# Byte offsets of the rounded products' operands, and the down products in two groups (spectral filter and mixture of experts, one core)

## The chip, the cores and the metric

The kernel runs on one core of one Trainium2 chip. The metric is the time of one execution on the device in microseconds (us), as the median of several runs. TensorE (PE) multiplies; its weight loads (PEld) run beside its matmuls. VectorE (DVE), ScalarE (ACT) and GpSimd (POOL) work on tiles, and SyncE (SP) issues most transfers.

## The reference, cut to what matters

```
X = rfft(x, axis=1)                        # x: 8 batches x 2496 rows x 256
Yr = Xr @ w_r - Xi @ w_i + b_r             # Xr, Xi: real and imaginary part of X
Yi = Xr @ w_i + Xi @ w_r + b_i
Yr, Yi = soft_threshold(Yr, 0.01), soft_threshold(Yi, 0.01)
x = irfft(Yr + 1j * Yi, n=2496, axis=1)    # then 19968 tokens of 256
logits = x @ w_gate                        # 8 experts
e = argmax(logits); g = softmax(logits)[e]
out = g * (relu(x @ w1[e]) @ w2[e])        # w1: 256 x 1024, w2: 1024 x 256 per expert
```

## The kernel before, in words

The first 540 us are the spectral part. The transform of length 2496 = 39 x 64 is made of two short ones, both as matmuls. For each of 8 batches and 10 steps, `fwd_a` makes the first half of the forward transform, `fwd_b` the second, `mix` multiplies by `w_r`, `w_i - w_r` and `-w_i - w_r`, `inv_b`, `inv_z` and `inv_y` go back, and `gate_z`, `gate_y` and `route` choose an expert for each token and send its row to a list in memory. The rest is the expert part: 82 tiles of 256 tokens, each with an up product (`up`, L1081) and a down product (`down`, L1117 to L1120).

Products that must be more exact than one pass of rounded numbers gives are made of three: an operand is split into a rounded part (`h`, made by ACT in type float32r) and the rest (`l`, made by DVE), and PE adds up h·h, l·h and h·l. These are the **rounded products**. The ones with 256 moving columns are called narrow here, those with 512 wide:

- `mix` (L404): 18 narrow matmuls a step in 80 steps, 1440 in all. Weights of PE are `sh`, `sl`; the moving operands are `wh*`, `wl*`.
- `fwd_a` (L336): 3 wide for each of 66 pieces. Weights `fah`, `fal` (and `feh`, `fel`), moving `xah`, `xal`.
- `inv_y` (L491): 3 wide for each of 88 pieces. Weights `gh`, `gl`, moving `zh`, `zl`.
- `up`: 48 narrow a tile, in 4 groups of 12. Weights `h1`, `l1`, moving `xh2`, `xl2`. ACT then makes `hh` of a group, and DVE `hl`.
- `down`: two halves of 128 tokens (`h`), and in each, for 8 pieces `f`, one wide matmul that multiplies `hh` by both halves of `h2` (rounded and rest, 2 x 256 columns) and one narrow that multiplies `hl` by the rounded half. They stand alternately, the narrow one a piece behind.

Tiles are placed by pools, in the order in which the code asks for them, so a tile's byte offset in a partition follows from the sizes of those ahead of it. The order of PE, ACT, DVE and SP is the order of the code (a hand-written schedule in `spectral` and `finish_last`, then `step` tile after tile in `experts_rest`). Where a tile has a new expert, ACT and DVE split its weights first (`split1`, `split2`).

Of the kernel before, what the change touches and what calls it, by code (L numbers as in the profile page):

```python
# [10 lines left out]
F32 = mybir.dt.float32  # L11
# [88 lines left out]
class Kernel:  # L100
# [33 lines left out]
    def pool(self, st, name, bufs, side="left", **kw):  # L134
        return st.enter_context(self.tc.tile_pool(name=name, bufs=bufs, side=side, reuse_waits="tile", **kw))

    def open_inverse(self, st, pst):
        nc, nb = self.nc, self.nb
# [22 lines left out]
        self.gar = k.tile([120, 117], F32, name="gar")  # L161
        self.gh = k.tile([120, 117], F32R, name="gh")
        self.gl = k.tile([120, 117], F32R, name="gl")
        self.ids = k.tile([117, nb, G], I32, name="ids")
# [7 lines left out]
        self.mark = k.tile([1, 1], F32, name="mark")  # L172
        self.zf = [k.tile([128, 5288], F32, name=f"z{i}") for i in range(2)]
        self.zs = [z[:, 0:5280].rearrange("p (c n a) -> p c n a", c=2, n=66) for z in self.zf]

    def open_forward(self, st):
        tc, nc, nb = self.tc, self.nc, self.nb
        f = self.f = self.pool(st, "f", 1, side="right")
        self.xst = ExitStack()
        self.xp = self.pool(self.xst, "xp", 3)  # L180
        self.xh, self.xl = {}, {}
        self.tp = self.pool(st, "tp", 6, side="right")
# [18 lines left out]
        nc.sync.dma_start(self.fer, self.c_fe)  # L201
        self.wh, self.wl = {}, {}
        self.raw = {}
        self.nlam = f.tile([128, 1], F32, name="nlam")
# [42 lines left out]
    def split_weights(self):  # L247
        nc, f, raw = self.nc, self.f, self.raw
        ws = self.w.tile([128, 2, D], F32, tag="r", name="wsum")
        wd = self.w.tile([128, 2, D], F32, tag="r", name="wdif")  # L250
        raw["d"], raw["s"] = wd, ws

        def split(nm):
            self.wh[nm] = f.tile([128, 2, D], F32R, name="wh" + nm)
            self.wl[nm] = f.tile([128, 2, D], F32R, name="wl" + nm)
            nc.scalar.copy(self.wh[nm], raw[nm])
            nc.vector.tensor_sub(self.wl[nm], raw[nm], self.wh[nm])

        split("r")
        nc.vector.tensor_sub(wd, raw["i"], raw["r"])  # L260
        split("d")
        nc.scalar.copy(self.bias.rearrange("p a d -> p (a d)"), self.pbias)
        nc.vector.scalar_tensor_tensor(out=ws, in0=raw["i"], scalar=-1.0, in1=raw["r"], op0=ALU.mult, op1=ALU.subtract)
        split("s")
# [35 lines left out]
    def split_first(self):  # L300
        nc = self.nc
        self.fhl = []
        for nm, src in (("fa", self.far), ("fe", self.fer)):
            h = self.xp.tile(list(src.shape), F32R, name=nm + "h", bufs=1)
            l = self.xp.tile(list(src.shape), F32R, name=nm + "l", bufs=1)
            nc.scalar.copy(h, src)
            nc.vector.tensor_sub(l, src, h)
            self.fhl.append((h, l))
# [615 lines left out]
    def open_weights(self):  # L924
        self.xst.close()
        k2 = self.k2 = self.pool(self.top, "k2", 1)
        k2.tile([128, 144], F32, name="even")
        self.r1 = [k2.tile([128, F], F32, name=f"r1{q}") for q in range(2)]
# [116 lines left out]
    def upright(self, t):  # L1045
        if t >= self.nt:
            return
        nc = self.nc
        xf = self.w2p.tile([128, 2, 8, 32], F32, tag="xf", name="xf")
        nc.vector.transpose(xf.rearrange("p c t j -> p t c j"), self.xqs.pop(t))  # L1050
        yield
        xf = xf.rearrange("p c t j -> p c (t j)")
        xh = self.w2p.tile([128, 2, TT], F32R, tag="xh2", name="xh2", bufs=2)
        xl = self.w2p.tile([128, 2, TT], F32R, tag="xl2", name="xl2", bufs=2)
        with self.tc.high_priority():
            nc.scalar.copy(xh, xf)
        yield
        with self.tc.high_priority():
            nc.vector.tensor_sub(xl, xf, xh)
        self.xts[t] = (xh, xl)  # L1060

    def up(self, t, work=()):
# [4 lines left out]
        if t and self.psb:  # L1067
            self.split2(t)
        hh = self.w2p.tile([128, 8, TT], F32R, tag="hh", name="hh")
        hl = self.w2p.tile([128, 8, TT], F32R, tag="hl", name="hl")  # L1070
        for f2 in range(4):
# [26 lines left out]
    def down(self, t):  # L1098
# [9 lines left out]
        else:  # L1108
            at = [xr.bitcast(I32)[:, h, 1:2] for h in range(2)]
        o = self.w2p.tile([128, 2, D], F32, tag="o", name="o", bufs=2)  # L1110
        for h in range(2):
            p = self.psb.tile([128, 512], F32, tag="o", name="po") if self.psb else \
                self.psi.tile([128, 512], F32, tag="u", name="po", bufs=4)
            hs = slice(h * 128, (h + 1) * 128)
            for f in range(8):
                if f:
                    nc.tensor.matmul(p[:, :D], hl[:, f - 1, hs], w2[:, f - 1, 0, :], start=False, stop=False)  # L1117
                if f == 7:
                    nc.tensor.matmul(p[:, :D], hl[:, 7, hs], w2[:, 7, 0, :], start=False, stop=False)
                nc.tensor.matmul(p, hh[:, f, hs], w2[:, f].rearrange("p a d -> p (a d)"), start=f == 0, stop=f == 7)  # L1120
                if f == 3 and t < 2:
                    yield
            if not h:
# [67 lines left out]
```

## Time and profile before

| | |
|---|---|
| median of 3 runs | 1485.34 us (1484.37 to 1485.68) |
| profiled execution | 1484.46 us, its span 1482.6 us |
| PE busy | 1460.2 us, 98% of the span |
| DVE, ACT, POOL busy | 932.8, 772.3, 480.0 us |

A row of a timeline gives the start, the length, the engine, the line, the operation and its tiles, written as out<-in; for a matmul the first name after the arrow is the moving operand and the second PE's weights. Numbers at the ends of names are left out, so `h` stands for `h1` or `h2`, and `l` for `l1`. Matmuls overlap, so the time that one takes from PE is the step from its start to the next start, not its length.

### The profile page before, as it was taken

The numbers are of one execution on the slowest core, as the hardware profiler recorded it, in microseconds if no ns is written. First come the engines' busy times: TensorE is split into PE (matmuls) and PEld (weight loads), VectorE is DVE, ScalarE is ACT, GpSimd is POOL, SyncE is SP. The second block draws the span as 40 slices with busy tenths as digits, with TensorE's granted clock in tenths as the row PEclk, the third lists the DMA queues.
The fourth block names the chain that finished last, engine by engine and source line by source line (L and its number), as shares of the span: only waits on it lengthen the run. The fifth ranks groups of instructions, "written<-read, shape, count | busy, mean of one in ns | idle before, by whom it ended". The sixth has DMA issues, their size and how long they took to land. (4 is left out here: it accounts for less than half of the span.)

```text
span 1482.6 us, 34736 instructions
## 1 busy us (share of the span) xinstructions
PE 1460.2 (98%) x10551; PEld 1325.4 (89%) x10552; DVE 932.8 (63%) x1951; ACT 772.3 (52%) x1537; POOL 480.0 (32%) x594
## 2 busy tenths in 40 slices
PE   8999999999999999999999999999999999999997
PEld 4889898898988878999999999999999999999996
DVE  3788898988989876455455545455545445445443
ACT  2778787887877763344343434334334334334332
POOL 3042565666665353334221111111112111111111
PEclk9999999999999999999999999999999999999999
DMA  7974565565645334244342323323223213232210
GB/s 228 255 220 123 150 177 164 164 177 159 176 129 152 71 104 120 69 130 124 99 115 55 100 68 88 74 69 103 53 52 91 55 47 98 55 74 65 53 43 21
DMA packets 194336, 161.97 MB, mean 109 GB/s; under 512 B 128011, under 2 KB 164531, under 8 KB 194128
## 3 DMA queue, kind: packets, MB, share of 16 engines
q1 hardware_dynamic: 173616, 113.37, 30.2%
q0 software_dynamic: 20512, 46.20, 9.3%
q8 instruction: 86, 1.41, 0.4%
q14 instruction: 122, 1.00, 0.2%
HBM read 241.99 MB, written 66.37 MB: 208 GB/s over the span
## 5 line engine op out<-in xcount | busy, mean ns | idle before, releaser
L1120 PE MATMUL po<-h,hh 128*128 128x512 f32 x1312 | 461.7, 394 | 0.0
L1081 PE MATMUL ph<-xh,h 128*128 128x256 f32 x1312 | 366.4, 279 | 0.0
L1081 PE MATMUL ph<-xl,h 128*128 128x256 f32 x1312 | 366.0, 279 | 0.0
L1081 PE MATMUL ph<-xh,l 128*128 128x256 f32 x1312 | 365.9, 279 | 0.0
L1117 PE MATMUL po<-h,hl 128*128 128x256 f32 x1148 | 324.6, 283 | 1.2 <-DVEq L1031 0.6
L1087 DVE SCALAR_TENSOR_TENSOR hl<-ph,hh 128x512 fp32r<-128x512 f32 x328 | 225.8, 689 | 135.9 <-ACT hh L1086 115.5
L1129 POOL DMA_INDIRECT out<-o,row x124 | 123.3, 994 | 573.9 <-DVE o L1127 465.3
L1086 ACT ACTIVATE hh<-ph 128x512 fp32r<-128x512 f32 x328 | 193.6, 597 | 187.1 <-PE ph L1081 185.2
L1120 PEld LDWEIGHTS po<-h,hh 128*128 128x128 f32 x1312 | 241.1, 188 | 43.4 <-issue 0.4
L1127 DVE SCALAR_TENSOR_TENSOR o<-po,xr,part 128x256 f32<-128x256 f32 x156 | 75.4, 483 | 301.1 <-ACT part L1126 151.8
L1081 PEld LDWEIGHTS ph<-xh,l 128*128 128x128 f32 x1312 | 246.8, 188 | 3.8
L1126 ACT ACTIVATE part<-po,xr 128x256 f32<-128x256 f32 x156 | 73.8, 473 | 335.0 <-PE po L1120 332.7
L1081 PEld LDWEIGHTS ph<-xh,h 128*128 128x128 f32 x1312 | 246.5, 188 | 0.5 <-issue 0.3
L1081 PEld LDWEIGHTS ph<-xl,h 128*128 128x128 f32 x1312 | 246.7, 188 | 0.0
L1117 PEld LDWEIGHTS po<-h,hl 128*128 128x128 f32 x1148 | 215.6, 188 | 9.4 <-DVE hl L1087 4.1
L822 POOL DMA_INDIRECT xs_dram<-yb,pos x176 | 177.8, 1010 | 59.5 <-issue 47.8
L438 DVE SCALAR_TENSOR_TENSOR y<-v,r 64x256 f32<-64x256 f32 x320 | 133.6, 417 | 5.7 <-ACT r L432 0.6
L458 ACT COPY z<-pv 128x256 f32<-128x256 f32 x160 | 93.8, 708 | 0.1
L761 POOL COPY mark<-y 1x1 f32<-1x1 f32 x72 | 25.3, 351 | 205.8 <-DVE y L438 205.5
L454 PE MATMUL pv<-bi,y 128*128 128x128 f32 x640 | 86.8, 277 | 3.2 <-DVE y L438 3.1
L371 PEld LDWEIGHTS pb<-bm,t 128*128 128x128 f32 x640 | 78.4, 191 | 10.4 <-DVE mx L778 3.4
L371 PE MATMUL pb<-bm,t 128*128 128x128 f32 x640 | 86.6, 278 | 0.8 <-DMA t<-spec_dram 0.8
(206 smaller groups left out, 2544.9 us busy)
## 6 DMA issues: line engine op xcount, KB each, us to landing
r<-moe_w SPq DMA_DIRECT2D x672, 128.0 KB
r<-moe_w SPq DMA_DIRECT2D x166, 512.0 KB
xq<-xs_dram SPq DMA_DIRECT2D x332, 64.0 KB
t<-spec_dram SPq DMA_DIRECT2D x160, 128.0 KB
spec_dram<-ae SPq DMA_DIRECT2D x77, 240.0 KB
x<-x SPq DMA_DIRECT2D x38, 384.0 KB
x<-x SPq DMA_DIRECT2D x38, 84.0 KB
xs_dram<-yb,pos POOLq DMA_INDIRECT x176, 3.0
```

The lines of the kernel that those rows point to most:

```text
L371: nc.tensor.matmul(p[:, c, :, kp, :], t[:, kp, c * 128:(c + 1) * 128], self.bm[:, 2 * s + kp, :], start=True, stop=True)
L438: nc.vector.scalar_tensor_tensor(out=y[q * 64:q * 64 + 64, kp, :], in0=u[h, q, :], scalar=LAM, in1=r[h, q, :], op0=ALU.add, op1=ALU.min)
L454: nc.tensor.matmul(p[:, c, kp, :, :], y[:, kp, c * 128:(c + 1) * 128], self.bi[:, 2 * s + kp, :], start=True, stop=True)
L458: nc.scalar.copy(self.zs[b % 2][:, c, 0:NB, 4 * s:4 * s + 4].rearrange("p n a -> p a n"), p[:, c].rearrange("p a r n -> p (a r) n"))
L822: i = nc.gpsimd.indirect_dma_start(out=self.xs[:, :], out_offset=bass.IndirectOffsetOnAxis(ap=pos[:n, g:g + 1], axis=0), in_=y[:n, g, :], ...
L1081: nc.tensor.matmul(p[:, i, :], a[:, c, f * 128:(f + 1) * 128], v[:, c, :], start=m == 0, stop=m == 5)
L1086: nc.scalar.activation(hh[:, s, :], p, AF.Relu)
L1087: nc.vector.scalar_tensor_tensor(out=hl[:, s, :], in0=p, scalar=0.0, in1=hh[:, s, :], op0=ALU.max, op1=ALU.subtract)
L1117: nc.tensor.matmul(p[:, :D], hl[:, f - 1, hs], w2[:, f - 1, 0, :], start=False, stop=False)
L1120: nc.tensor.matmul(p, hh[:, f, hs], w2[:, f].rearrange("p a d -> p (a d)"), start=f == 0, stop=f == 7)
L1127: nc.vector.scalar_tensor_tensor(out=o[:, h, :], in0=p[:, :D], scalar=xr[:, h, 0:1], in1=part, op0=ALU.mult, op1=ALU.add)
L1129: i = nc.gpsimd.indirect_dma_start(out=self.out[:, :], out_offset=bass.IndirectOffsetOnAxis(ap=at[h], axis=0), in_=o[:, h, :], in_offset=N ...
```

## The change

A helper `skip` asks a pool for a tile that nothing uses, and so moves what comes after it. Eight such tiles are placed, `gh`, `gl` and the parts of `far` and `fer` get rows of 128 columns (512 bytes) of which the first 117 or 120 are used, and the split weights of `mix` are asked for ahead of `nlam`. The old tile `even` (576 bytes) becomes one of 544. What this does to the start of each operand, as the two built programs have it, in bytes mod 256:

```
product      moving operand          PE's weights
             before    after         before            after
mix          224       192           0 (sh, sl)        0
fwd_a        0         0             128, 96, 64, 32   0
inv_y        96        192           192 (gh) 160 (gl) 192
up           224       192           192 (h1, l1)      0
down wide    224       0             160 (hh)          0
down narrow  224       0             160 (hl)          64
```

So in the kernel after, a wide product's weights start at the same offset as its moving operand, and a narrow product's weights 64 bytes behind it (mod 256). Before, the differences are 32 (mix), 128 to 32 (fwd_a), 96 and 64 (inv_y), 224 (up) and 192 (down).

In `down`, the 16 matmuls of a half are put in another order: first the 8 wide ones, then the 8 narrow ones.

```diff
+    def skip(self, pool, n):
+        pool.tile([128, n // 4], F32, name=f"skip{n}", bufs=1)
...
-        self.gh = k.tile([120, 117], F32R, name="gh")
-        self.gl = k.tile([120, 117], F32R, name="gl")
+        self.gh = k.tile([120, 128], F32R, name="gh")[:, 0:117]
+        self.gl = k.tile([120, 128], F32R, name="gl")[:, 0:117]
...
         self.zf = [k.tile([128, 5288], F32, name=f"z{i}") for i in range(2)]
+        self.skip(k, 32)
...
         self.xp = self.pool(self.xst, "xp", 3)
+        self.skip(self.xp, 32)
...
         self.wh, self.wl = {}, {}
+        for nm in "rds":
+            self.wh[nm] = f.tile([128, 2, D], F32R, name="wh" + nm)
+            self.wl[nm] = f.tile([128, 2, D], F32R, name="wl" + nm)
...
-            h = self.xp.tile(list(src.shape), F32R, name=nm + "h", bufs=1)
-            l = self.xp.tile(list(src.shape), F32R, name=nm + "l", bufs=1)
+            m, n = src.shape
+            h = self.xp.tile([m, 128], F32R, name=nm + "h", bufs=1)[:, 0:n]
+            l = self.xp.tile([m, 128], F32R, name=nm + "l", bufs=1)[:, 0:n]
...
-        k2.tile([128, 144], F32, name="even")
+        self.skip(k2, 544)
...
+        if not t:
+            self.skip(self.w2p, 192)
         xh = self.w2p.tile([128, 2, TT], F32R, tag="xh2", name="xh2", bufs=2)
...
+        if not t:
+            self.skip(self.w2p, 128)
         hh = self.w2p.tile([128, 8, TT], F32R, tag="hh", name="hh")
+        if not t:
+            self.skip(self.w2p, 64)
         hl = self.w2p.tile([128, 8, TT], F32R, tag="hl", name="hl")
...
+        if t == self.early:
+            self.skip(self.w2p, 96)
...
             for f in range(8):
-                if f:
-                    nc.tensor.matmul(p[:, :D], hl[:, f - 1, hs], w2[:, f - 1, 0, :], start=False, stop=False)
-                if f == 7:
-                    nc.tensor.matmul(p[:, :D], hl[:, 7, hs], w2[:, 7, 0, :], start=False, stop=False)
-                nc.tensor.matmul(p, hh[:, f, hs], w2[:, f].rearrange("p a d -> p (a d)"), start=f == 0, stop=f == 7)
-                if f == 3 and t < 2:
-                    yield
+                nc.tensor.matmul(p, hh[:, f, hs], w2[:, f].rearrange("p a d -> p (a d)"), start=f == 0, stop=False)
+            if t < 2:
+                yield
+            for f in range(8):
+                nc.tensor.matmul(p[:, :D], hl[:, f, hs], w2[:, f, 0, :], start=False, stop=f == 7)
```

The order on PE, at the second half of one expert tile's down product and the start of the next tile's up product. Before:

```order
L1120 MATMUL po<-h_8033,hh 128x512 x2
L1117 MATMUL po<-h_8033,hl 128x256
L1120 MATMUL po<-h_8033,hh 128x512
L1117 MATMUL po<-h_8033,hl 128x256
L1120 MATMUL po<-h_8033,hh 128x512
L1117 MATMUL po<-h_8033,hl 128x256
```

and so on, until the half ends:

```order
L1117 MATMUL po<-h_8033,hl 128x256
L1119 MATMUL po<-h_8033,hl 128x256
L1120 MATMUL po<-h_8033,hh 128x512
L1031 UNCONDITIONAL_BRANCH
L1081 MATMUL ph<-xh_12545,h_7220 128x256
L1081 MATMUL ph<-xh_12545,l_7221 128x256
L1081 MATMUL ph<-xl_12546,h_7220 128x256
```

The last wide one of the first half and the first of the second half are the only two wide ones in a row (the x2). After the change, both halves and the start of the next tile:

```order
L1131 MATMUL po<-h_8035,hh 128x512 x8
L1135 MATMUL po<-h_8035,hl 128x256 x8
L1131 MATMUL po<-h_8035,hh 128x512 x8
L1135 MATMUL po<-h_8035,hl 128x256 x8
L1038 UNCONDITIONAL_BRANCH
L1094 MATMUL ph<-xh_14213,h_7222 128x256
L1094 MATMUL ph<-xh_14213,l_7223 128x256
L1094 MATMUL ph<-xl_14214,h_7222 128x256
```

The number of matmuls is the same. A wide one now follows a wide one in 14 of 16 cases, and a half's last narrow one comes last. Rows of ACT, DVE and POOL stand in the same order as before. On SP one load of expert weights at the start of the expert part waits for PE in addition, for a matmul of the last `mix`.

## Rows read from the trace of the kernel before

**Rows 1.** The page, parts 1 and 2: TensorE's total and its granted clock.

```profile
PE 1460.2 (98%) x10551; PEld 1325.4 (89%) x10552; DVE 932.8 (63%) x1951; ACT 772.3 (52%) x1537; POOL 480.0 (32%) x594
PEclk9999999999999999999999999999999999999999
```

**Rows 2.** Two stretches: their us, then busy PE, PEld, DVE, ACT, POOL; granted clock.

```profile
100.00:400.00 300.00, 300.00 (x2331) 272.00 (x2328) 265.20 (x625) 236.87 (x513) 170.07 (x205) 1.00 0.58 166
630.00:1482.00 852.00, 842.28 (x5982) 785.97 (x5980) 425.97 (x750) 336.51 (x612) 170.03 (x184) 1.00 0.29 75
```

**Rows 3.** Timeline of TensorE, one expert tile and the next one's start.

```profile
1000.90 0.28 PE L1081 MATMUL ph<-xh,h 128*128 128x256 f32 x1
...
1006.51 0.39 PE L1120 MATMUL po<-h,hh 128*128 128x512 f32 x1
1006.74 0.28 PE L1117 MATMUL po<-h,hl 128*128 128x256 f32 x1
...
1008.96 0.28 PE L1119 MATMUL po<-h,hl 128*128 128x256 f32 x1
1009.07 0.62 PE L1120 MATMUL po<-h,hh 128*128 128x512 f32 x2
1009.53 0.28 PE L1117 MATMUL po<-h,hl 128*128 128x256 f32 x1
...
1012.12 0.28 PE L1081 MATMUL ph<-xh,h 128*128 128x256 f32 x1
```

**Rows 4.** Matmul lengths by line: count, min/median/max in ns, first and last start.

```profile
L1081 PE MATMUL ph<-xh,h x1312: 277/280/388, 532.4 to 1467.0; 128*128 128x256 f32 x188
L1081 PE MATMUL ph<-xl,h x1312: 276/280/285, 532.7 to 1467.3; 128*128 128x256 f32 x188
L1120 PE MATMUL po<-h,hh x1312: 387/394/502, 544.4 to 1472.8; 128*128 128x512 f32 x188
L1117 PE MATMUL po<-h,hl x1148: 276/282/392, 544.7 to 1472.5; 128*128 128x256 f32 x192
L404 PE MATMUL pk<-wlr,sh x160: 277/281/288, 33.1 to 518.6; 128*128 128x256 f32 x160
L491 PE MATMUL py<-zh,gh x88: 390/400/494, 104.2 to 557.0; 120*117 120x512 f32 x88
L491 PE MATMUL py<-zh,gl x88: 388/392/400, 104.4 to 557.2; 120*117 120x512 f32 x88
```

**Rows 5.** The same for two kinds of matmul that are not rounded products.

```profile
L700 PE MATMUL pw<-first x51: 378/379/634, 1.5 to 28.8; 128*128 128x512 bf16 x51
L371 PE MATMUL pb<-bm,t x640: 270/275/377, 29.9 to 510.6; 128*128 128x128 f32 x160
```

**Rows 6.** Timeline of TensorE: the bias products of L400 in two places.

```profile
508.16 0.28 PE L400 MATMUL pm<-bias_r,ones 128*128 128x256 f32 x1
508.29 0.28 PE L404 MATMUL pm<-whd,sh 128*128 128x256 f32 x1
...
508.99 0.28 PE L400 MATMUL pm<-bias_r,ones 128*128 128x256 f32 x1
509.11 0.28 PE L404 MATMUL pm<-whs,sh 128*128 128x256 f32 x1
```

**Rows 7.** One down product with a late weight load, on ACT, DVE, PE and PEld.

```profile
837.39 1.08 ACT L1086 ACTIVATE hh<-ph 128x512 fp32r<-128x512 f32 x2
...
839.22 0.68 DVE L1087 SCALAR_TENSOR_TENSOR hl<-ph,hh 128x512 fp32r<-128x512 f32 x1
...
839.54 0.40 PE L1120 MATMUL po<-h,hh 128*128 128x512 f32 x1
839.96 0.19 PEld L1117 LDWEIGHTS po<-h,hl 128*128 128x128 f32 x1 [0.35 <-DVE hl L1087]
```

**Rows 8.** The waits of weight loads: us in total, times, longest.

```profile
PEld po L1117 <- DVE hl L1087: 4.1, 11, 0.5
```

**Rows 9.** Last products of the spectral part; the issue of expert weights on SP.

```profile
520.40 0.28 PE L404 MATMUL pm<-whs,sl 128*128 128x256 f32 x1
524.24 5.66 SPq L994 DMA_DIRECT2D r<-moe_w  x10
```

More of the change, by code (lines that the diff above doesn't have):

```diff
@@ L247, in split_weights @@
     def split_weights(self):
-        nc, f, raw = self.nc, self.f, self.raw
+        nc, raw = self.nc, self.raw
         ws = self.w.tile([128, 2, D], F32, tag="r", name="wsum")
@@ L253, in split @@
         def split(nm):
-            self.wh[nm] = f.tile([128, 2, D], F32R, name="wh" + nm)
-            self.wl[nm] = f.tile([128, 2, D], F32R, name="wl" + nm)
             nc.scalar.copy(self.wh[nm], raw[nm])
```

## The prediction

> **What bounds the kernel now.** I read the page first. TensorE is busy 98% of the span and its granted clock is at the top (2.4 GHz) in all 40 slices [rows 1]. The stretches come next: in the expert part, 852 us from 630 on, PE is busy 842 us, DVE and ACT 426 and 337; in the spectral part PE has no idle time between 100 and 400 us, but DVE is busy 265 of 300 us there [rows 2]. So only time on PE counts, in the expert part one for one, in the spectral part as far as DVE follows.
>
> What does a matmul take? The timeline answers by steps from start to start. One tile's 48 up matmuls run from 1000.90 to 1006.51: 5.61/48 = 0.1169 us a step. Its 32 down matmuls run to 1012.12: 5.61/16 = 0.351 us for a wide and a narrow one together [rows 3]. The median lengths are 0.280 (up), 0.394 (wide) and 0.282 us (narrow) [rows 4]; 0.280 less 0.1169 leaves 0.163, and with this taken off, wide and narrow are 0.231 and 0.119, together 0.350, as the timeline has it. So step = length - 0.163 us, and differences between lengths are differences between steps.
>
> Now the comparison on which the change stands. The bf16 matmul with 512 columns is 0.379 long, a step of 0.216. The one of L371, plain float32 with 128 columns, is 0.275, a step of 0.112 [rows 5]; at 2.4 GHz that is 269 cycles, and a narrow rounded matmul with its 256 columns should need about as many. A rounded wide one needs 0.231 for the same 512 columns, a narrow one 0.117 to 0.119. So 15 ns of a wide and 5 to 7 ns of a narrow one are not columns. They are no fixed price: the same matmul on the same tiles varies, wide from 0.387 up, narrow from 0.276 up [rows 4]; `zh` with `gh` has a median of 0.400 and with `gl` 0.392 [rows 4]. Something between the streams of reads varies, and the start offsets are one thing that could set it.
>
> **The change, part by part.** The number of matmuls and the work of ACT, DVE and POOL stay. The unused tiles cost no instruction.
>
> *Offsets.* No row shows all operands at the new offsets, so I bound the effect. Best case: every rounded product gets the step of [rows 5]. Up: 3936 x (280 - 275) ns = 19.7 us. Wide: 1312 x (394 - 379) = 19.7. Narrow of `down`: 1312 x (282 - 275) = 9.2. In the spectral part 1440 `mix` matmuls x (281 - 275) = 8.6 and 462 wide ones (264 of `inv_y`, 198 of `fwd_a`) x 17 (the mean of 400 and 392, less 379) = 7.9; together 16.5, of which I count half, as DVE is busy 88% there. Sum 48.6 + 8.3 = 56.9 us. Worst case: the new offsets are bad ones; a narrow step becomes 0.120 (below, among the rivals), and the up products lose 3936 x 3 ns = 12 us. Between these far ends I take the nearest rows, the shortest that the same matmuls reach in this trace: up 277, wide 387, narrow 276, `mix` 277, `inv_y` 390 and 388 [rows 4]. Up 3936 x 3 = 11.8; wide 1312 x 7 = 9.2; narrow 1312 x 6 = 7.9; spectral 1440 x 4 = 5.8 and 462 x 7 = 3.2, half of both 4.5. Sum 33.4 us.
>
> *Groups of eight.* The only two wide ones in a row take 0.46 together, so 0.23 each, and the narrow L1119 that follows a narrow one takes 0.11 to 0.12 [rows 3]. At 0.230 and 0.117 a tile's down product would be 16 x 0.347 = 5.55 instead of 5.61, 0.06 us less, 82 times: 4.9 us. This is the part of the gain that doesn't need the offsets; it is contained in the 33.4, not added.
>
> *A wait that goes.* In 11 tiles, those with a new expert, the load of `hl` for the seventh narrow matmul waits for DVE [rows 8]. The step there is 839.96 - 839.54 = 0.42 instead of 0.23 [rows 7]: 11 x 0.19 = 2.1 us. `hl` is ready at 839.90. The seventh wide one starts six pairs after the down product, so that began at 839.54 - 6 x 0.35 = 837.44, and `hl` comes 2.46 us into it. In the new order its load can go after 8 wide and 6 narrow ones, at 8 x 0.224 + 6 x 0.113 = 2.47. The wait is gone. What is asked for sooner is the last pair of `hh`: the seventh wide one now comes after 6 x 0.224 = 1.34 us; ACT has it at 837.39 + 1.08 = 838.47, 1.03 us in [rows 7]. Margin 0.3 us; without it each of the 11 tiles would pay the difference.
>
> *The load on SP* that waits for one more matmul of the last `mix`: those start until 520.40, and SP issues expert weights from 524.24 on [rows 9]. Nothing; if PE were later than SP there, the loads behind it would move by the same amount.
>
> Sum: 33.4 + 2.1 = 35.5 us off the profiled execution's 1484.5 gives 1449.0. That execution is 0.9 us under the median of the three runs, so I say **1450 us**.
>
> **The rivals.**
>
> *Offsets do nothing* (25%). In [rows 7] the weight load behind a wide matmul starts 0.42 us after it, so nothing is loaded while it runs; it is 0.40 long all the same, no shorter than the 0.394 of those with a load beside them. This speaks against a conflict between both reads, which is what a difference between offsets could cure. So does [rows 6]: while the bias product of L400 runs, its moving operand starts at 192 and the weights being loaded at 0, the pair that `mix` and `up` shall have; its steps are 0.13 and 0.12, not 0.112. Left are the groups and the wait, 4.9 + 2.1 = 7 us: 1478.
> The Trainium skill says the same in "TensorE: Matmul & The Clock Gate", section "Step-by-step: what each phase is for": the array has one read port for the moving operand and another for weight loads, and loading the next weights takes no read bandwidth from the running matmul; by that rule the time would be this rival's. The wide matmul without a load beside it agrees; that the lengths vary on the same tiles does not fit so well.
>
> *All of the excess goes* (17%): 56.9 + 2.1 = 59 us, 1426; with all of the spectral part 1418. For it speaks that 0.112 and 0.216 are reached by products that read half the bytes in the same time. Against it, that no rounded product of this trace gets there: 0.387 is 8 ns above 0.379.
>
> *Slower* (16%). The weights of narrow products are put 64 bytes behind the moving operand. If that is a bad difference, a step becomes that of the first bias product, 0.12 to 0.13 [rows 6], against 0.1169 in `up`, which now runs very evenly. At 0.120 `up` loses 12 us and `mix` nothing; the groups and the wait give 7 back: 1490. It decides from 0.1187 on, where `up` alone eats the 7 us.
>
> **How the numbers follow.** Likeliest, at 42%: the shortest lengths of the trace become the rule, 1450. The range takes in the rival without an effect of offsets (1478, and up to 1486 if the groups don't help either) and most of the full gain: 1420 to 1486. I leave out some 5% below it and 12% above. A measurement of this kernel can tell 0.2%, 3 us. Faster than that: 42 + 17 + 15 of the 25 (the other 10 for groups that give less than 3 us) = 74%. Same: 10%. Slower: 16%.
>
> **What would show it.** In the profile after, the median lengths of the up matmul (277 forecast, 275 at full gain, 280 without an effect, 283 when slower), of the wide (387, 379, 393) and narrow ones of `down` (276, 275, 280); a tile of 10.85 us instead of 11.22 between starts of up products; in the late tiles no wait for `hl` and none for `hh`. The spectral part should end 3 to 6 us sooner; if its matmuls shorten and its end stays, DVE holds it. I am wrong if the lengths do not move, or if they fall in one product and rise in the other: then the differences of 0 and 64 bytes are not both good ones.

## The result, and the profile after

The changed kernel takes 1466.15 us (median of 4 runs, 1464.89 to 1468.46) against 1484.86 us before (1484.29 to 1485.68): a ratio of 0.9875, interval 0.9858 to 0.9892. So 18.7 us went, about half of the 35 us that were forecast. The time lies inside the range on record and 16 us above the number on record.

First the page of the kernel after, its span, part 1 and the clock of part 2:

```profile
span 1463.5 us, 34966 instructions
PE 1440.6 (98%) x10552; PEld 1308.7 (89%) x10552; DVE 932.2 (64%) x1951; ACT 775.0 (53%) x1537; POOL 481.3 (33%) x594
PEclk9999999999999999999999999999999999999999
```

Against [rows 1], PE is busy 19.6 us less, with one matmul record more; the work of the other engines and the clock are nearly as they were. The span lost 1482.6 - 1463.5 = 19.1 us, which PE's busy time accounts for. The expert part from 630 us on, to set beside the second line of [rows 2]:

```profile
630.00:1460.00 830.00, 823.38 (x5956) 771.12 (x5955) 424.05 (x747) 336.68 (x609) 170.07 (x182) 1.00 0.30 77
```

The matmul lengths by line (count, min/median/max in ns, first and last start):

```profile
L1094 PE MATMUL ph<-xh,h x1312: 276/276/387, 530.5 to 1447.9; 128*128 128x256 f32 x188
L1131 PE MATMUL po<-h,hh x1312: 387/389/501, 542.5 to 1452.7; 128*128 128x512 f32 x188
L1135 PE MATMUL po<-h,hl x1312: 276/281/388, 545.4 to 1453.7; 128*128 128x256 f32 x188
L411 PE MATMUL pk<-wlr,sh x160: 276/281/283, 33.6 to 516.8; 128*128 128x256 f32 x160
L498 PE MATMUL py<-zh,gh x88: 390/398/488, 104.3 to 555.0; 120*117 120x512 f32 x88
L498 PE MATMUL py<-zh,gl x88: 387/392/400, 104.6 to 555.3; 120*117 120x512 f32 x88
```

Beside [rows 4] the reader sees three different fates. The up product has come to the 276 ns that was its shortest before, at the median. The wide ones of `down` have a median of 389 after 394. The narrow ones of `down`, which share the difference of 64 bytes with the up product, still stand at 281 after 282. The first up product starts at 530.5 instead of 532.4.

A median hides what stands in a row, so here is one tile on TensorE, with the next one's start:

```profile
990.60 0.28 PE L1094 MATMUL ph<-xh,h 128*128 128x256 f32 x1
...
996.06 1.99 PE L1131 MATMUL po<-h,hh 128*128 128x512 f32 x8
997.89 1.11 PE L1135 MATMUL po<-h,hl 128*128 128x256 f32 x8
998.83 2.00 PE L1131 MATMUL po<-h,hh 128*128 128x512 f32 x8
1000.67 1.11 PE L1135 MATMUL po<-h,hl 128*128 128x256 f32 x8
1001.61 0.28 PE L1094 MATMUL ph<-xh,h 128*128 128x256 f32 x1
```

The up part takes 996.06 - 990.60 = 5.46 us instead of the 5.61 of [rows 3], a step of 0.1138. The down part takes 5.55 instead of 5.61: eight wide in 1.83 and 1.84 us, 229 to 230 ns each, and eight narrow in 0.94, 117.5 each. The tile has gone from 11.22 to 11.01 us.

From the starts of all matmuls, mean step in ns (steps that a late operand stretched, over 245 ns for a wide and 130 for a narrow one, left out; the wait for `hl` is taken from the ten tiles with a new expert from 690 us on, the late tiles here: what they take beyond the others, 2.88 us before and 2.35 after):

```
                 before    after    times   gives us   forecast us
up               116.8     113.8    3936      11.9       11.8
wide of down     231.7     229.3    1312       3.1        9.2
narrow of down   118.8     117.7    1312       1.5        7.9
wait for hl                                    0.5        2.1
first up product starts at 532.4, 530.5        1.9        4.5
```

These sum to 18.9 of the span's 19.1 us.

### The profile page after: what moved, and what is told of

The parts are those of the page before. It is cut to its first block, busy times and chain, and to the rows that moved or that the text cites. A ratio compares the mean times of both kernels' runs of the same rounds, so it can differ in the third digit from the quotient of the medians.

```text
span 1463.5 us, 34966 instructions
## 1 busy us (share of the span) xinstructions
PE 1440.6 (98%) x10552; PEld 1308.7 (89%) x10552; DVE 932.2 (64%) x1951; ACT 775.0 (53%) x1537; POOL 481.3 (33%) x594
## 5 line engine op out<-in xcount | busy, mean ns | idle before, releaser
L1131 PE MATMUL po<-h,hh 128*128 128x512 f32 x1312 | 329.0, 392 | 1.3 <-ACT hh L1099 0.6
L1131 PEld LDWEIGHTS po<-h,hh 128*128 128x128 f32 x1312 | 233.7, 188 | 45.7 <-ACT hh L1099 2.5
L1135 PEld LDWEIGHTS po<-h,hl 128*128 128x128 f32 x1312 | 178.7, 189 | 14.4 <-DVE hl L1100 0.7
L1135 PE MATMUL po<-h,hl 128*128 128x256 f32 x1312 | 183.8, 282 | 0.0
```

What stands on the lines that cost most here:

```text
L1135: nc.tensor.matmul(p[:, :D], hl[:, f, hs], w2[:, f, 0, :], start=False, stop=f == 7)
```

## The experiments

**The table of starts.** In this kernel nothing but TensorE works beside the preparation of its operands. It runs chains of 24 equal matmuls, for 8 starts of the moving operand (tiles `ma` to `mh`) and 8 of the weights (outputs `pa` to `ph`, 0 to 224 bytes mod 256):

```
for c in "abcdefgh":                   # moving start 0, 32, ... 224
    for j, d in enumerate("abcdefgh"): # weights start 0, 32, ... 224
        for i in range(24):
            nc.tensor.matmul(p[d][:, 0:256], w[:, 8 * j:8 * j + 128], m[c][:, 0:256], start=i == 0, stop=i == 23)
```

Then the same with 512 columns, and chains in which either operand or both step from matmul to matmul by multiples of 1024 bytes.

> This kernel computes nothing of the reference: it runs chains of 24 rounded matmuls on one operand pair after another, first 256 columns wide (8 starts of the moving operand, 0 to 224 bytes mod 256 in steps of 32, times 8 starts of the weights), then 512 wide, then narrow ones whose operands step from one matmul to the next as in a down product (moving 2048 bytes, weights 1024), then with only the moving operand or only the weights stepping (moving start 0, weights 0 to 224). Theory A, the difference weights minus moving mod 256 sets the step: all chains with one difference agree within 1 ns; narrow 113 ns at 64 and 117 at 224, wide 227 at 0 and above 229 at 192. Theory B, the moving operand's own start sets it (multiples of 64 bytes good, odd multiples of 32 bad): narrow 113 for moving starts 0, 64, 128, 192 and 117 for 32, 96, 160, 224, whatever the weights' start. Theory C, what counts is whether operands are used again: chains without steps 113, the stepping ones 118, at every start.

The mean step of the chains' last 15 steps, by the difference (weights minus moving, mod 256), eight chains to a difference:

```
difference      0      32     64            96     128    160    192    224
wide (ns)      226.7  233.5  233.5         234.2  233.6  233.3  228.9  233.2
narrow (ns)    120.0  118.5  113.3, 117.8  117.3  118.7  120.2  117.8  117.8, 116.7
```

Whatever the single starts are, nearly all chains with one difference agree: what counts in the first place is the difference. One wide chain at 128 stands 1.3 ns below the other seven. Four narrow differences hold chains apart from the rest by about a ns or more: at 64, two chains run at 113.3 and six at 117.8; at 224, two run at 116.7 to 116.9; at 96, the two that follow the short ones at 64, and at 128 one, stand at 120.0. Rows of the wide chains at 0, 64 and 192, then of narrow ones at 64, two long and two short (lengths; a step is 163 ns less):

```profile
L51 PE MATMUL pa<-ma,w x24: 388/389/397, 193.6 to 198.8; 128*128 128x512 f32 x24
L51 PE MATMUL pc<-ma,w x24: 393/396/398, 204.6 to 210.0; 128*128 128x512 f32 x24
L51 PE MATMUL pg<-ma,w x24: 388/392/398, 227.1 to 232.3; 128*128 128x512 f32 x24
...
L46 PE MATMUL pc<-ma,w x24: 281/281/283, 17.5 to 20.2; 128*128 128x256 f32 x24
L46 PE MATMUL pd<-mb,w x24: 281/281/283, 43.0 to 45.7; 128*128 128x256 f32 x24
L46 PE MATMUL pg<-me,w x24: 276/276/283, 119.7 to 122.4; 128*128 128x256 f32 x24
L46 PE MATMUL pb<-mh,w x24: 276/276/286, 173.7 to 176.3; 128*128 128x256 f32 x24
```

The same instruction with the same difference is 276 ns long in one chain and 281 in another, from the fifth step to the last but one. Narrow chains whose operands step do not differ from those that stay: a step that is a multiple of 256 bytes changes nothing. What follows: the offsets act through the difference, and at 64 a narrow chain has two lengths, so the difference doesn't settle it.

**The parts of the change alone.** First the up product's starts alone, in the kernel before (three unused tiles, moving at 192 and weights at 0; `down` as before):

```diff
-        k2.tile([128, 144], F32, name="even")
+        self.skip(k2, 640)
...
+        if not t:
+            self.skip(self.w2p, 224)
         xh = self.w2p.tile([128, 2, TT], F32R, tag="xh2", name="xh2", bufs=2)
...
+        if not t:
+            self.skip(self.w2p, 32)
         hh = self.w2p.tile([128, 8, TT], F32R, tag="hh", name="hh")
```

> The kernel before, with the new starts for the operands of the up product alone (moving 192, weights 0); all else at the old starts, in the old order. Theory A and B: the up matmul falls from 280 to 276 or 277 ns, 3936 x 3.3 ns = 13 us, the down product as before: ratio 0.991. Rival (the up product gains because the down product ahead of it leaves another phase behind): the up matmul stays at 280, ratio 1.000.

Measured: 1479.82 us, ratio 0.9962 (0.9948 to 0.9975), 5.6 us. The up step is 115.1, not 113.8: in most tiles the up part takes 5.46 us, in some 16 of 71 it takes 5.65. Those tiles run at the longer of the two lengths from beginning to end. One of each, the start of the up part and of the down part:

```profile
886.97 0.28 PE L1088 MATMUL ph<-xh,h 128*128 128x256 f32 x1
...
892.43 0.39 PE L1127 MATMUL po<-h,hh 128*128 128x512 f32 x1
...
1389.36 0.28 PE L1088 MATMUL ph<-xh,h 128*128 128x256 f32 x1
...
1395.01 0.40 PE L1127 MATMUL po<-h,hh 128*128 128x512 f32 x1
```

The 16 are not scattered: each row of long tiles begins right behind a late tile, in which a late `hl` stretched a step (seven of the ten), and the last row, ten of the 16, runs on to the end. So even the up product's gain needs what runs ahead of it. That a wait there can cost it is read from where the long tiles stand; no run tried it.

Second, the order of `down` alone, on the starts of before, which is the diff's last part without the rest:

> The kernel before, with the down product in groups of eight wide and eight narrow, all starts as before. If the order by itself helps: wide after wide at 0.230 and narrow after narrow at 0.117, 5 us, and up to 2 us of waits: ratio 0.995. Theory A (at the difference of 192 the groups settle at a bad step, wide 233): ratio 0.999 to 1.002.

Measured: 1476.92 us, ratio 0.9945 (0.9931 to 0.9959), 8.2 us by the ratio. One of its tiles:

```profile
1002.59 1.99 PE L1116 MATMUL po<-h,hh 128*128 128x512 f32 x8
1004.42 1.11 PE L1120 MATMUL po<-h,hl 128*128 128x256 f32 x8
1005.36 2.00 PE L1116 MATMUL po<-h,hh 128*128 128x512 f32 x8
1007.20 1.07 PE L1120 MATMUL po<-h,hl 128*128 128x256 f32 x8
1008.11 0.28 PE L1081 MATMUL ph<-xh,h 128*128 128x256 f32 x1
```

The second eight narrow ones take 0.91 us where the first take 0.94. In 42 of 81 tiles the second eight have a mean step of 113.9 ns, in the others 117.5 to 118.1, and from the eleventh tile on this changes only in a late tile or right behind one. Their difference is 192, at which all chains of the table stood at 117.8: so the short length is not peculiar to 64. Third, all the starts with the old alternating order:

> The kernel after, with the down product in the old alternating order: all starts new. Up 13 us and spectral part 2 us as in the kernel after; the down product without its groups as in the kernel before: 15 us, ratio 0.990. If the new starts help the down product in the old order too: 0.986 or less. If they hurt it there (a wide one's moving operand meets a narrow one's weights at a difference of 64): 0.993.

Measured: 1471.92 us, ratio 0.9913 (0.9899 to 0.9926), 12.9 us. The mean steps of the three beside the others, in ns:

```
                     up      wide    narrow of down   mix
before               116.8   231.7   118.8            118.2
up's starts alone    115.1   231.7   118.9            118.2
order alone          116.8   229.6   116.8            118.2
starts alone         113.9   232.7   116.7            115.8
all (the change)     113.8   229.3   117.7            115.8
```

In the order of groups, the new starts of `down` change wide by -0.3 ns and narrow by +0.9: 1312 x 0.6 = 0.8 us more. So what `down` gained is the grouping's; its new starts gave nothing on top. The means of the order alone are themselves a mixture: in its quiet tiles the down part takes 5.52 us in one state and 5.57 in the other, and 5.55 in the changed kernel.

**Is it the other engines?** TensorE alone plays the tile: 48 narrow, then `down`, five tiles for each of 24 settings of the starts.

> Only TensorE works here, on rows of x in place of every operand; all of the reference's work is left out. It plays the tile of the experts' part without waits: 48 narrow products (the up product) and 32 of the down product, five tiles for each setting, 24 settings. Settings a to h of the first and the second group move the start of hl by 0, 32, ... 224 bytes (so that is the difference of the starts in the narrow products of down; the wide ones stand at 0); the first group runs eight wide and eight narrow twice, the second sixteen wide and then sixteen narrow. The third group moves the start of xh and xl instead (the up product's difference runs 0, 224, 192, ... 32), with hl at 64. Theory A (a chain at difference 64 has two lengths, 113.3 and 117.8 ns a step, and what ran before picks one): at hl 64 in the first group the up product runs at about 113.5 and the narrow ones of down at about 117.7, as in the changed kernel, though nothing but TensorE works; some other setting of hl, or the run of sixteen, gives 116.5 or less in the narrow ones of down. Theory D (the 117.7 comes from what the other engines do beside the down product: SBUF reads and writes by ScalarE, VectorE and the transfers): with these silent the narrow ones of down at 64 fall to 113.5 as the up product's do. In both, the wide ones need four or so to settle at 226.7, so that sixteen in a row come to 227.9 on the mean and eight to 229.2.

Rows of the setting that stands for the changed kernel (hl at 64, eight and eight), the up product first:

```profile
L57 PE MATMUL upc<-xh,lup x80: 276/276/283, 122.5 to 171.9; 128*128 128x256 f32 x80
...
L65 PE MATMUL dpc<-w,hh x80: 387/389/398, 128.0 to 176.5; 128*128 128x512 f32 x80
L69 PE MATMUL dpc<-w,hl x80: 280/281/282, 129.9 to 177.5; 128*128 128x256 f32 x80
```

They are the medians of the changed kernel, 276, 389 and 281, though ScalarE, VectorE and the transfers are silent. Theory D falls. The steps of one such tile show how the chain settles: the up product 119, 121, 116, 114, 114, 113, 113, 114 and so on at 113.3; the first eight wide 232, 232, 231, 227, 226, 227, 227, 226; the narrow ones 118, 117, 118, 117, 119, 117, 118, 118 from the first on. In the changed kernel's trace the same series stands. The three to five steps behind each change of product are what keeps eight wide ones at 229 when the table says 226.7. No start of `hl` in the eight settings brought both the narrow ones of `down` under 117 and the up product under 114; theory A's expectation of 116.5 or less in some setting failed (the lowest is 116.6, with the up product at 117.8).

**Sixteen wide, sixteen narrow.** The changed kernel with one change of product in `down` in place of three:

```diff
-        for h in range(2):
...
+        apart = self.psb and t > 1
...
+        if apart:
+            wide(0)
+            wide(1)
+        for h in range(2):
+            if not apart:
+                wide(h)
```

> The changed kernel with sixteen wide products and then sixteen narrow ones per tile from the third tile on, where both of the tile's PSUM buffers are there. Theory A (the wide ones pay for each entry from narrow ones): one entry per tile in place of two; the second group of eight wide stands at 226.7 from its start, so it gains the transient once, (231.7 - 226.7) x 4 = 20 ns a tile, and one of two entries of the narrow ones, some 0 to 10 ns: 80 tiles, 2 us, ratio to before 0.986, faster than the changed kernel by 0.0010 to 0.0020. In the tiles in which hl is late, its wait falls: the sixteen wide take 3.66 us and hl is done 2.62 us into the down product, so the two late steps of 0.24 and 0.22 us go as well, at most 2 x 0.1 us in some 20 tiles, 4 us: together 0.983 to 0.986. The rival theory (the four long ones at the head of each eight come from the first half's eviction or from the late weight load, not from the entry): no gain in the wide ones beyond the hl wait. Against a gain: the first half's eviction on ScalarE and VectorE now begins 1.8 us later, beside the second's; the out transfers follow it, and if the next tile's buffers wait for it, up to 0.3 us a tile is lost, ratio 0.99 or above.

Measured: ratio to before 0.9841 (0.9827 to 0.9854). The wide step is 228.0 instead of 229.3, the narrow one still 117.8, and the down part of the tiles with a new expert takes 5.53 to 5.57 us instead of 5.77 to 5.79. The new order holds from the eighth tile on, in 75 tiles, not from the third as the expectation has it. The transient belongs to the change of product, and the late `hl` is covered by eight more wide matmuls.

**What sets the state.** TensorE alone again; now the first block of `hl` (f = 0) alone is moved, so that one step at the head of the narrow chain is odd.

> TensorE alone again, on rows of x in place of every operand, none of the reference's work: five tiles for each of 24 settings, up product at difference 64, wide ones of down at 0, narrow ones of down at 64. What is moved is the first block of hl alone (f = 0), to a start of 0, 32, ... 224 bytes (settings a to h), so that the narrow chain is entered by an odd step. First group: sixteen wide, then the narrow ones with the two halves in turn (two odd steps, each moving block used twice running). Second: sixteen wide, then eight and eight narrow, one odd step. Third: eight wide and eight narrow twice, as in the changed kernel, one odd step for each eight. Theory A (the state is set at the entry and then kept): the up product goes into the short state because its first step has difference 0 against the narrow one ahead of it; so an odd step of 0 (setting a), and perhaps others, brings the narrow chain of down to 113.5 ns in place of 117.9, in the second group by 15 x 4.4 = 66 ns a tile; setting c (64, no odd step) stays at 117.8. Rival E (it isn't the entry but the up product's own pattern, in which a moving block is used twice running or a chain starts anew every six): then all settings of the second and the third group stay near 117.8, and the first group comes down to about 113.5 in setting c too if it is the moving block used twice.

Mean steps in ns of the second group (sixteen and sixteen, one odd step), tiles two to five of each setting:

```
start of the first block    0      32     64     96     128    160    192    224
narrow of down             113.3  117.8  117.9  117.8  114.6  113.5  117.9  118.3
up                         117.8  113.7  113.7  113.7  117.8  117.8  113.7  113.7
```

The lengths of the settings 0 and 64, for the up product and the two kinds of narrow block in `down`:

```profile
L57 PE MATMUL uqa<-xh,lup x80: 281/281/283, 455.4 to 505.2; 128*128 128x256 f32 x80
...
L71 PE MATMUL dqa<-w,hl x75: 276/276/278, 464.7 to 510.8; 128*128 128x256 f32 x75
L71 PE MATMUL dqa<-w,hk x5: 276/276/276, 464.6 to 509.1; 128*128 128x256 f32 x5
...
L57 PE MATMUL uqc<-xh,lup x80: 276/276/283, 566.2 to 615.3; 128*128 128x256 f32 x80
...
L71 PE MATMUL dqc<-w,hl x75: 280/281/283, 575.3 to 620.9; 128*128 128x256 f32 x75
```

One odd step at difference 0 brings all fifteen others of the narrow chain from 281 to 276, and the up product, which nobody touched, goes from 276 to 281. In every setting of this group one of the two is short and the other long. So the state is carried from chain to chain, and one step at 0, 128 or 160 turns it over; the first step of the up product is such a step, since its weights start at 0 and the moving block ahead of it too. In the first group, where two steps at 0 follow each other, the narrow chain is 113 for one step and then back at 117.6, the up product at 113.7: two turns cancel. At the other starts of this group they don't: at 32, 128, 160, 192 and 224 the up product stands at 117.8 and the narrow chain at 113.6 to 115.2, though one step at 32, 192 or 224 turned nothing. So that two steps cancel is shown for 0 alone, and no simple count of turns covers the eight starts. Theory A holds as far as this goes. Rival E falls, since an entry alone does it.

**The state in the real kernel.** The run of sixteen, with `hl`'s first block at 0 and the others at 64; the second half takes that block last:

```diff
-        hl = self.w2p.tile([128, 8, TT], F32R, tag="hl", name="hl")
+        hlf = self.w2p.tile([128, 8 * TT + 16], F32R, tag="hl", name="hl")
+        hl = hlf[:, 16:].rearrange("p (f t) -> p f t", t=TT)
+        hl01 = hlf[:, 0:2 * TT + 32].rearrange("p (f t) -> p f t", f=2)[:, :, 0:TT]
...
+            fs = [1, 2, 3, 4, 5, 6, 7, 0] if apart and h else range(8)
```

> Sixteen wide and sixteen narrow products per tile as in the run of sixteen, with the first block of hl (f = 0) at start 0 and the other seven at 64: the narrow chain is entered by one step at difference 0, runs f = 1 to 7 of both halves at 64, and is left by the second half's f = 0, again at 0, on to the up product, whose first step is at 0 as before. Theory A (a step at difference 0 carries the chain at 64 over between its two lengths, 113.3 and 117.8, and two of them in a row cancel, as the settings with the first block alone moved show): the fourteen steps run at 113.5 in place of 117.8, about 14 x 4.3 = 60 ns a tile; the two odd steps at the exit and the up product's entry cancel, so the up product stays at 113.8; 78 tiles, 4.7 us less than the run of sixteen, ratio to before 0.981. Rival F (the exit doesn't cancel: the up product changes places with the narrow chain and runs at 117.8): minus 4.7 us and plus 48 x 4.1 ns x 78 = 15 us, 10 us slower than the run of sixteen, ratio 0.991. Rival E (the state is nothing that carries over in the real kernel, where late steps and other engines come between): ratio 0.984, as the run of sixteen.

Measured: ratio 0.9832 (0.9818 to 0.9846). The narrow step falls to 113.8 and the up product stays at 114.1; rival F's exchange, 117.8 for the up product, did not come in the tiles of sixteen. In the seven tiles ahead of them, with an odd step at the head of each eight and none behind, it did: the up part takes 5.65 us in the fourth and the sixth to eighth tile, where the run of sixteen has 5.46. That is what setting 0 of the entry run shows for groups of eight (117.8). The time alone could not tell it from the run of sixteen, which ran on another chip; the last three runs do.

**The spectral starts undone** in the changed kernel, the expert part's kept:

```diff
-        self.gh = k.tile([120, 128], F32R, name="gh")[:, 0:117]
+        self.gh = k.tile([120, 117], F32R, name="gh")
...
-        self.skip(k, 32)
...
-        self.skip(k2, 544)
+        self.skip(k2, 640)
```

> The changed kernel with the starts of the spectral products (those of the two transforms, of the mixing and their weights) as before the change; all starts of the experts' part and the grouping stay. It prices the spectral term of the forecast, 4.5 us. By the two traces the first up product of the changed kernel begins 1.9 us earlier, and the steps of the mixing sum to 3.1 us less, of the forward transform to 0.4 more, of the inverse to none. Theory A (step set by the difference of the starts): 1466 + 1.9 to 2.7 us, ratio to before 0.9888 to 0.9893 against 0.9875 of the changed kernel. Rival (the 1.9 us are how the stage's transfers fell, not its starts): ratio 0.9875. The forecast's term: 0.9905.

Measured: ratio 0.9886 (0.9869 to 0.9902), 1.6 us more than the changed kernel's 0.9875, with intervals that overlap: a tendency. Its `mix` step is back at 118.2, its `fwd_a` at 233.2 (234.5 with the new starts), `inv_y` is 232.2 in both. The term of 4.5 us, 0.9905, lies outside the interval.

**Three kernels side by side** on one chip:

> The changed kernel once more, so that the next two stand beside it on one chip: ratio to before 0.9875, as measured, on any chip, if the length of a step depends on starts and order alone; up product 113.8 a step, narrow ones of down 117.7, wide 229.3.

> Sixteen wide, then sixteen narrow, again. From its trace: 75 tiles took 824.9 us against 829.1 of the changed kernel, 4.2 us less, 3 us of it the late hl in the tiles that change the expert: ratio to the changed kernel 0.997, to before 0.9845.

> The run of sixteen with the odd step in front of the narrow chain and behind it, again. From its trace: 75 tiles took 821.1 us, 3.9 us less than the run of sixteen and 8.1 less than the changed kernel: ratio to the changed kernel 0.9945, to before 0.982. If the state of the narrow chain were an accident of one chip, its ratio would be that of the run of sixteen.

Measured, before at 1484.93 us there: the changed kernel 1465.95 us, ratio 0.9875 (0.9860 to 0.9890); the run of sixteen 1461.31, 0.9847 (0.9833 to 0.9860); with the odd step 1458.28, 0.9820 (0.9807 to 0.9834). A tile's down product in the run of sixteen:

```profile
992.91 3.80 PE L1134 MATMUL po<-h,hh 128*128 128x512 f32 x16
996.55 2.05 PE L1148 MATMUL po<-h,hl 128*128 128x256 f32 x16
```

and with the odd step, and the next up product's start:

```profile
993.87 3.80 PE L1134 MATMUL po<-h,hh 128*128 128x512 f32 x16
997.51 1.98 PE L1150 MATMUL po<-h,hl 128*128 128x256 f32 x16
999.33 0.29 PE L1094 MATMUL ph<-xh,h 128*128 128x256 f32 x1
```

The wide ones take 3.64 us in both. The narrow ones take 2.05 us to the end of the last in the one, 1.98 in the other, 0.07 us a tile; 75 times that is 5 us, of which the median shows 3.0. Part of the rest goes in the first tiles, where the up product runs long, and part in new waits, in tiles with a new expert. The weight loads of the wide ones, waits in us, times and longest, with the odd step:

```profile
PEld po L1134 <- ACT hh L1099: 3.2, 8, 0.7
PEld po L1134 <- ACTq L1038: 2.8, 12, 0.8
```

In the run of sixteen these two are 2.1 and 1.4 us. So ScalarE's `hh` is late next; that it is so because PE is quicker still is argued, not tried. This is the fastest kernel of the study, 26.7 us under before.

## Why the prediction was right, and where it was not

**What bounds the kernel** was read rightly. PE's busy time fell by 19.6 us and the span by 19.1; in the expert part it is still busy 823 of 830 us, and DVE and ACT 424 and 337.

**Up, 11.8 us:** measured 11.9. That the shortest lengths of the trace would become the rule held here, and in part by luck: the prediction knew of no state. By the entry run it holds because the up product's first step turns the chain into the short one; with `down` ahead of it in the old order and at its old starts, 16 of 71 tiles missed it, and the starts of the up product alone gave 5.6 us.

**Narrow of down, 7.9 us: this is the step that failed most.** "The shortest that the same matmuls reach in this trace" was taken for what the new starts would make the rule. They were lengths that single matmuls reach between others (276). At 64 bytes there are two lasting lengths, and behind the wide ones the chain stays in the longer, 281. The term gave 1.5 us, and by the runs of the parts that came with the grouping. The step by which it could have been had, one odd block, wasn't in the change.

**Wide of down, 9.2 us:** measured 3.1, and most of it not by the starts. The table has 226.7 at difference 0 and 228.9 at 192, the difference before, so the starts themselves were worth 2.2 ns at best. In the kernel the order alone brought 2.1 of the 2.4 ns (231.7 to 229.6), the new starts the last 0.3; in the old order they made the wide ones longer (232.7). So for `down` the forecast put down to the starts what the grouping did. Each group of eight pays 231 to 236 for its first three to five steps. [rows 4]'s shortest, 387 less 163 = 224, is below what a chain at 0 settles at in the table.

**Groups of eight** were put at 4.9 us as the part that needs no offsets. The run with the order alone gave 8.2 us, its interval 6.1 to 10.2. The up product was as before there, so `down` had it all: its narrow ones reached 116.8 and its wide ones 229.6, and in eight of the ten late tiles the down part is 0.04 to 0.14 us longer than in the tiles ahead of them, where before it was 0.26 in most.

**The wait for hl, 2.1 us,** hardly went: 0.5 us came of it. The eleven waits of [rows 8] are not eleven tiles either. Three fall in the first ten tiles of the stage and eight in the ten late tiles behind them, and the late tiles lost 0.26 us or more each, since the step behind the late one is long too (0.22 instead of 0.12): 2.9 us in all. One such tile of the kernel after, rows of PE, ACT and DVE:

```profile
774.99 2.02 PE L1131 MATMUL po<-h,hh 128*128 128x512 f32 x8
775.09 1.08 ACT L1099 ACTIVATE hh<-ph 128x512 fp32r<-128x512 f32 x2
775.71 0.69 DVE L1100 SCALAR_TENSOR_TENSOR hl<-ph,hh 128x512 fp32r<-128x512 f32 x1 [0.61 <-ACT hh L1099]
776.32 0.68 DVE L1068 TENSOR_TENSOR xl<-xf,xh 128x512 fp32r<-128x512 f32 x1
...
776.85 1.31 PE L1135 MATMUL po<-h,hl 128*128 128x256 f32 x8
776.92 0.69 DVE L1100 SCALAR_TENSOR_TENSOR hl<-ph,hh 128x512 fp32r<-128x512 f32 x1
...
778.00 2.00 PE L1131 MATMUL po<-h,hh 128*128 128x512 f32 x8
```

The eight narrow ones take 778.00 - 776.85 = 1.15 us instead of 0.94; the 0.21 lost stand where 0.19 were counted before. The step at fault is the 2.46 us at which `hl` was to come. It was counted from the start of the down product, and the up product got 0.15 us shorter while the work of DVE did not: `hl` ends at 776.92 + 0.69 = 777.61, which is 2.62 us into the down product. A faster stage ahead uses up the slack of the one behind. The runs of the parts bear this out from both sides. With the order alone the up product was as long as before, and the wait was down to 0.04 to 0.14 us in eight of ten such tiles. With the up product 0.14 us shorter and the old order (its starts alone, and all starts alone), the late tiles take 0.41 us or more beyond the others instead of 0.26. Of `hh`, ACT has the last pair at 776.17, 1.18 us in, before the seventh wide one at 1.4: no wait in this tile, as forecast. In the first ten tiles of the stage the loads now wait for `hh` where they waited for `hl`. The waits of the wide ones' loads for `hh`, before and after:

```profile
PEld po L1120 <- ACT hh L1086: 0.2, 1, 0.2
...
PEld po L1131 <- ACT hh L1099: 2.5, 5, 1.0
```

**Spectral, 4.5 us:** the stage ended 1.9 us sooner, and undoing its starts cost 1.6, a tendency. In the runs of the parts, on one chip, the first up product starts at 533.1 and 533.4 us with the old spectral starts and at 530.5 with the new. `mix` gained 2.4 ns a step and `fwd_a` lost 1.4, although its differences are now 0. Its wide ones stand three in a row, and three is what the wide chain of `down` needs to settle; that this is the reason is argued, not tried.

**The rivals.** "Offsets do nothing" falls: the same wide product with the same data costs 226.7 or 233.5 ns, by the difference alone. Both rows that spoke for it can be read otherwise. The bias product of [rows 6] is one matmul between others, and a chain's first steps at difference 64 are 119, 121, 116 where it goes on at 113.3. The wide one of [rows 7] follows a narrow one, and such a one has 231 to 233 at difference 0 as well, in the tile played by TensorE alone. Why it was no shorter without a weight load beside it is open: no run held the load back.
The Trainium skill, "TensorE: Matmul & The Clock Gate", section "Step-by-step: what each phase is for", gives the moving operand and the weight loads a read port each and has them not disturb one another; the table of starts does not fit that, since a wide step there changes by up to 7.5 ns with where the two start, and the measurement decides.
"All of the excess goes" was half possible: a narrow chain comes to 113.3, 1.3 ns above the 112 of [rows 5]; a wide one gets no lower than 226.7 where bf16 takes 216. "Slower" put 120 ns on the difference 64; 120.0 is the price of 0, and 120.2 of 160.

**Open:** what the state is. The runs show that a difference of 64 has two lasting lengths, and that a step at 0 turns one into the other. They don't show the mechanism, nor why the second eight of the order alone reach the short length at 192, nor which late steps turn the state.

## What to carry to other kernels

Where a matmul's step is longer than its columns explain, run short chains of it alone for each start mod 256 of both operands: the difference decides most of it, and it costs one run to know. Then test the chosen differences in the order in which the kernel has them, since the first steps behind a change of product are dearer, and a chain can stay in a state that its entry, or a late step before it, has set. The shortest length in a trace is what one matmul reached between its neighbours, and not what a row of them will.

## What the runs showed of the hardware that was not expected

- The step of rounded products depends on (weights' start minus moving start) mod 256 bytes: 226.7 to 234.2 ns for 512 columns, 113.3 to 120.2 for 256. In these chains the best difference is 0 for the wide and 64 for the narrow ones, and 0 is among the worst for the narrow.
- At 64 a narrow chain runs at 113.3 or at 117.8 ns for as long as it lasts. One step at difference 0, 128 or 160 on entering turned it over, and the chain behind it as well. At 192, the table's 117.8, groups of eight reached 113.9 in half of the tiles of the run with the order alone.
- In the run with the up product's starts alone, the length of a whole up product (5.46 or 5.65 us) changed, from the eleventh tile on, only behind tiles in which a late operand had stretched a step.
- In the changed kernel a group of eight wide matmuls needs three to five steps of 231 to 236 ns before it runs at 227; sixteen in a row bring the mean from 229.3 to 228.0.
